# Seven products for eight in a three-stage kernel: blocks 2 and 3 of the second network's first product, and one load queue

## Chip, cores and metric

The kernel runs on one core of a Trainium2 chip. The metric is the device time of one execution in microseconds (us). TensorE (PE) multiplies, VectorE (DVE) and ScalarE (ACT) work on tiles, SyncE (SP) issues transfers (DMAs), GpSimd (POOL) does almost nothing here.

## The reference

Attention with a threshold on 4 x 8 heads of 576 tokens and 64 columns, then two networks on the 2304 tokens of 512 columns. Cut to what is computed:

```python
scores = scale * np.matmul(q, k.transpose(0, 1, 3, 2))
thresh = np.max(scores, axis=-1, keepdims=True) - tau
scores = np.where(scores >= thresh, scores, -1000000000.0)
attn = softmax(scores)
x = (attn @ v)                       # 2304 x 512, float32
h = x @ w_in                         # first network, 512 -> 1024
solu = h * softmax(h)
x = (layernorm(solu) * g_ln) @ w_out # 1024 -> 512
h = x @ w_in2                        # second network, 512 -> 2048
g = np.maximum(h, 0.0) + np.log1p(np.exp(-np.abs(h)))
out = g @ w_out2                     # 2048 -> 512
```

All is float32. The kernel keeps that precision by splitting every operand of the networks into a high and a low part (float32r); a product is three matmuls: high x high, high x low, low x high.

## The kernel before

**Stages.** Attention goes over 32 pairs of heads and tiles of 128 queries: scores (L498), row maximum (L455), exponential (L456), mask with row sum (L458), transposes (L474), product with v (L533). Its result goes into `xr`. The first network goes over nine units of 256 tokens (L668, L726, L727) and stores each unit's result, high and low, to DRAM tensors `x2s` (L733). The weights w_in, w_out of the first network come as 64-bit words and are converted in `convert` by ScalarE (L590) and DVE (L591, L593, L594); for w_in the low half is taken by PE (L614, L615).

**Second network.** The tokens come in five blocks (L737): four of 512 tokens (units 0-1, 2-3, 4-5, 6-7) and one of 256 (unit 8). For each block `m2_load` brings the tokens back from `x2s`; then `m2_chunk` runs over 16 chunks `c` of 128 hidden columns: the first product is 4 parts of the contraction by 3 matmuls into one PSUM bank of tag `h2` (L775), then softplus in four steps on DVE and three on ScalarE (L786 to L792), the high and low half of the result, `gh` and `gl` (L793, L794), and the second product, 3 matmuls for each 128 tokens into the four banks `ys` (L798). With the last chunk `ys` is copied (L815, L817) and stored (L822). `prep_w2` converts the network's weights, one chunk at a time through two buffers `raw2`; `w2t` holds them.

**PSUM.** Eight banks: four of tag `w` and, once attention is over, four of tag `h2`.

**Order of the work.** Every operation is an entry of a plan with what it comes after and the buffers that it takes. For each engine the table `TURNS` lists the entries in the order in which they are issued. A waiting instruction holds up all behind it on its engine, on SP too. `filler` (L396) puts dummy matmuls on PE where a negative number stands in the table.

**Load queues.** `queue` (L410) sends the second half of q and k of pairs 0 and 1 over ScalarE's queue and every other load over SP's; the order on SP is the table's.

Of the kernel before, what the change touches and what calls it, by code (L numbers as in the profile page):

```python
# [957 lines left out]
```

## Time and profile before

| | us |
|---|---|
| median of 3 runs | 914.37 |
| lowest and highest | 912.44, 914.90 |
| the profiled execution | 912.48 |
| its span, first to last instruction | 910.7 |
| PE busy in the span | 894.5 |
| DVE, ACT busy | 689.0, 586.7 |

The span is what the trace covers; 1.8 us of the execution lie outside it. Matmuls are pipelined, so a busy PE is one that has a matmul in it, not one that works at its peak; what a matmul costs in a full stretch is the distance from one start to the next.

### The profile page before, as it was taken

What the parts mean: (1) busy time and instruction counts of PE and PEld (TensorE: products, weight loads), DVE (VectorE), ACT (ScalarE), POOL (GpSimd) and SP (SyncE); (2) the same over time, 40 slices, a digit from 0 to 9 for tenths busy, and PEclk for the clock granted to TensorE, in tenths of its full rate; (3) what the DMA queues carried; (4) which work ended last, traced back from release to release, by engine and by line L of the source; (5) the groups of instructions that cost most, each with busy time, mean ns of one, the idle gap of its engine ahead of it and who ended that gap; (6) DMA issues with size and microseconds to landing.
All of it is one profiled execution on the core that took longest, in us unless ns stands there. A gap on an engine that the chain in (4) does not pass through costs nothing.

```text
span 910.7 us, 14268 instructions
## 1 busy us (share of the span) xinstructions
PE 894.5 (98%) x5388; PEld 703.1 (77%) x5388; DVE 689.0 (76%) x1468; ACT 586.7 (64%) x1153; POOL 0.7 (0%) x6
## 2 busy tenths in 40 slices
PE   5999999999999999999999999999999999999998
PEld 4567776677777777788888888878888888888897
DVE  4899989887877787789879889986465655646566
ACT  4899978887867787757766656654353434444444
POOL 0000000000000000000000000000000000000000
PEclk8999999999999999999999999999999999999999
DMA  8704310131122000164323242431010200200001
GB/s 226 216 3 146 84 30 1 48 101 43 31 73 80 30 24 2 47 208 166 112 83 139 104 153 103 136 104 37 0 46 26 70 0 1 93 1 1 9 27 35
DMA packets 32052, 64.62 MB, mean 71 GB/s; under 512 B 3440, under 2 KB 12912, under 8 KB 31984
## 3 DMA queue, kind: packets, MB, share of 16 engines
q1 hardware_dynamic: 31520, 62.96, 21.5%
q8 instruction: 42, 0.69, 0.3%
q10 hardware_dynamic: 464, 0.75, 0.3%
q14 instruction: 26, 0.21, 0.1%
HBM read 49.55 MB, written 14.16 MB: 70 GB/s over the span
## 4 chain that ended last, share of the span: by engine, by line
PE 86%; DVE 6%; DMA 4%; ACT 3%; issue 1%; SPq 0%; ACTq 0%; DVEq 0%
PE h L775 18%; PE w L798 17%; PE w L668 11%; PE w L474 9%; PE w L533 8%; PE s L498 7%; PE w L726 7%; PE w L727 4%; PE w L709 2%; DMA k<-in_k_dram 1%; PE w L574 1%; DMA raw_out<-in_w_out_dram 1%; DMA raw<-in_w_in_dram 1%; PE w L512 1%; PE s L553 1%; DVE raw_out L593 1%
## 5 line engine op out<-in xcount | busy, mean ns | idle before, releaser
L775 PE MATMUL h<-x2m,w2h 128*128 128x512 f32 (+1 forms) x640 | 181.9, 368 | 0.0
L775 PEld LDWEIGHTS h<-x2m,w2h 128*128 128x128 f32 x640 | 116.8, 188 | 22.1 <-DVE gw L791 0.5
L455 DVE TENSOR_REDUCE nm<-s 128x1 f32<-128x576 f32 x144 | 103.9, 750 | 29.8 <-PE s L498 25.7
L775 PE MATMUL h<-x2m,w2l 128*128 128x512 f32 (+1 forms) x320 | 117.7, 368 | 0.0
L798 PE MATMUL w<-wo2h,gh 128*128 128x512 f32 x288 | 112.4, 390 | 0.5 <-DVE yo L817 0.5
L798 PE MATMUL w<-wo2l,gh 128*128 128x512 f32 x288 | 112.4, 390 | 0.0
L798 PE MATMUL w<-wo2h,gl 128*128 128x512 f32 x288 | 112.1, 389 | 0.0
L458 DVE SCALAR_TENSOR_TENSOR E<-E,etau 128x576 f32<-128x576 f32 x128 | 101.2, 812 | 9.6 <-ACT E L456 8.4
L477 ACT COPY eT<-w 128x512 f32<-128x512 f32 (+1 forms) x186 | 94.0, 544 | 21.9 <-PE w L474 20.8
L456 ACT ACTIVATE E<-s,nm 128x576 f32<-128x576 f32 x128 | 91.6, 747 | 19.7 <-DVE nm L455 19.0
L726 PE MATMUL w<-lhl,wo1h 128*128 128x512 f32 x288 | 103.9, 400 | 0.0
L790 ACT ACTIVATE gw<-gw 128x512 f32<-128x512 f32 (+1 forms) x80 | 47.0, 588 | 63.9 <-DVE t L789 63.5
L794 DVE TENSOR_TENSOR gl<-gw,gh 128x512 fp32r<-128x512 f32 (+1 forms) x80 | 50.8, 635 | 49.0 <-ACT gh L793 48.1
L474 PE MATMUL w<-ident,E 128*128 128x128 f32 x576 | 80.5, 279 | 4.9 <-DVE E L458 2.8
L498 PE MATMUL s<-k,q 64*128 64x288 f32 x512 | 82.5, 438 | 1.2 <-ACT q L424 0.8
L474 PEld LDWEIGHTS w<-ident,E 128*128 128x128 f32 x576 | 62.8, 140 | 26.7 <-issue 7.1
L786 ACT ACTIVATE t<-h 128x512 f32<-128x512 f32 (+1 forms) x80 | 43.9, 552 | 60.1 <-PE h L775 52.6
L793 ACT CAST gh<-gw 128x512 fp32r<-128x512 f32 (+1 forms) x80 | 45.8, 574 | 55.0 <-DVE gw L792 29.2
L727 PE MATMUL w<-lhl,wo1l 128*128 128x256 f32 x288 | 80.8, 280 | 0.0
L533 PE MATMUL w<-eT,v 128*64 128x256 f32 (+1 forms) x680 | 76.3, 371 | 0.0
L791 DVE SCALAR_TENSOR_TENSOR gw<-h,gw 128x512 f32<-128x512 f32 (+1 forms) x80 | 50.8, 636 | 31.0 <-ACT gw L790 30.4
L775 PEld LDWEIGHTS h<-x2m,w2l 128*128 128x128 f32 x320 | 60.2, 188 | 10.1
(107 smaller groups left out, 1544.9 us busy)
## 6 DMA issues: line engine op xcount, KB each, us to landing
x2s<-x SPq DMA_DIRECT2D x36, 256.0 KB, 2.1
x2m<-x2s SPq DMA_DIRECT2D x18, 512.0 KB, 4.9
raw_in<-in_w_in_dram SPq DMA_DIRECT2D x16, 512.0 KB, 3.7
raw_out<-in_w_out_dram SPq DMA_DIRECT2D x16, 512.0 KB, 3.5
v<-in_v_dram SPq DMA_DIRECT2D x16, 320.0 KB, 4.0
q<-in_q_dram SPq DMA_DIRECT2D x30, 144.0 KB, 3.1
raw<-in_w_out_dram SPq DMA_DIRECT2D x4, 1024.0 KB, 6.6
out_dram<-yo SPq DMA_DIRECT2D x15, 256.0 KB, 2.1
```

Of the source, the lines that this page charges most:

```text
L455: mx = op("DVE", 668, 750, lambda: dve.tensor_reduce(out=nm.t, in_=src(), axis=AX.XY, op=ALU.max, negate=True), after=[after], takes=[nm], ...
L456: ex = op("ACT", 638, 741, lambda: act.activation(out=dst().rearrange("p (a b) -> p a b", a=2), in_=src(), func=AF.Exp, bias=nm.t, scale=1.0),
L458: return op("DVE", 739, 900, lambda: dve.scalar_tensor_tensor(out=dst(), in0=dst(), scalar=etau, in1=dst(), op0=ALU.is_ge, op1=ALU.mult, a ...
L474: pe.transpose(bk.t[:, P * i:P * i + P], b_.t[:, c:c + P], ident)
L477: copies.append(op("ACT", occ, occ + 111, lambda: act.copy(out=eT.t[:, 0:width], in_=bk.t[:, 0:width]), after=[g], uses=[bk, eT]))
L498: pe.matmul(s[h].t[:, nh, 0:288], z["q"].t[r, c:c + P], z["k"].t[r, 288 * nh:288 * nh + 288], start=True, stop=True)
L533: pe.matmul(o_.t[64 * h:64 * h + 64, 0:W], z["v"].t[:, vcols(c, h)], e[8 if c == 8 else 4 * h + c](), start=(i == 0), stop=(i == 4))
L668: pe.matmul(ps.t, x__[:, part, :], w_[:, part, 512 * n:512 * n + 512], start=(part == 0 and j_ == 0), stop=(part == 3 and j_ == 2))
L726: pe.matmul(o.t.rearrange("p (a q) -> p a q", a=2), w1t["wo1h"][:, c, P * m:P * m + P], lhl.t[:, :, c, :], start=(c == 0), stop=False)
L727: pe.matmul(o.t[:, 0:256], w1t["wo1l"][:, c, P * m:P * m + P], lhl.t[:, 0, c, :], start=False, stop=(c == 7))
L775: pe.matmul(ps.t[:, 0:n], w2t["in", a, c][:, part, :], x.t[:, b_, part, 0:n], start=(part == 0 and j_ == 0), stop=(part == 3 and j_ == 2))
L798: pe.matmul(ys[j].t, g_.t[:, P * j:P * j + P], w2t["out", a, c], start=(c == 0 and i == 0), stop=(c == NC2 - 1 and i == 2))
```

## The change

**Seven products.** Blocks 2 and 3 (1024 tokens) are no longer taken one after the other. They and the two chunks c and c+8 form a 2 by 2 product in halves of the contraction (256 each). Eight products of such halves become seven, with sums of weights and sums of tokens as operands and five sums of the products behind them. A product is 2 parts by 3 matmuls (`product`). The seven use three `h2` banks, A, B and G: p1 and p2 in A; p6, p7, p4 in B; p5, p3 in G. A copy of p1 (`s1`) is added to B between its products, and results go to SBUF tiles `c22`, `c12` and back into `s1`: p7 comes after the add `u2`, p4 after `u3`, p3 after `c22`. Softplus reads A from PSUM and the other three from SBUF. The second product of block 2 runs beside it; block 3's results are kept in the places of used weights (`keep`) and its second product comes last.

**Sums.** `w2_sums` (DVE, ACT) makes four weight sums for each pair of chunks from the converted weights and stores them, high and low, to DRAM (`wsum`); in the product stage they are loaded again, two loads of 512 KB a pair, into the two `raw2` buffers. `x_sums` makes four token sums from `x2f`, an unsplit copy of the first network's result that units 4 to 7 now store too; one stays in SBUF, three go through `tsum` and come back into the places of weights of chunks 8 to 15 and of block 4's tokens.

**Order.** The blocks come as 0, 1, 4, then 2 and 3 together; block 4 takes its chunks as 8 to 15, then 0 to 7. `queue` sends only q of pair 0 over ScalarE's queue. `TURNS` is new throughout, and so are some constants by which the plan places operations (`LANDS`, `took`, a limit of eight loads under way). Nine tiles of one column (`m_...`) become one tile `few` of nine.

```diff
     def queue(what, i, h=0):
-        return "ACT" if what in "qk" and h and i < 2 else "SP"
+        return "ACT" if what == "q" and i == 0 else "SP"
...
+            if 4 <= u < 8:
+                full.setdefault(u - 4, []).append(load("SP", lambda u=u, m=m: x2f[u - 4][m], lambda xs_=xs_: xs_.t, 128, 1024, after=[s_], uses=[xs_]))
...
+    def four(name, fill, pairs):
+        x = buf("w2b", "sx", f"f_{name}", [P, 4, 256])
...
+        for o_, (i, a, b_, how) in enumerate(pairs):
+            last = [op("DVE", 343, 428, lambda i=i, a=a, b_=b_, how=how: dve.tensor_tensor(out=v(i), in0=v(a), in1=v(b_), op=how), after=last, uses=[x])]
...
+    def halves_of(x, after, into):
...
+            h_ = op("ACT", 110 + 424 * k_, 205 + 425 * k_, lambda src=src, hi=hi: act.copy(out=hi(), in_=src(x.t)), after=after, takes=[own] if new else (), uses=[x] + ([] if new else [own]))
+            got.append(op("DVE", 84 + 518 * k_, 165 + 526 * k_, lambda src=src, hi=hi, lo=lo: dve.tensor_tensor(out=lo(), in0=src(x.t), in1=f(hi()), op=ALU.subtract), after=[h_], uses=[x, own]))
...
+        x, last = four(f"w{c}", fill, [(3, 2, 3, ALU.add), (2, 0, 2, ALU.subtract), (0, 3, 0, ALU.subtract), (1, 1, 0, ALU.subtract)])
...
-    for bi in range(len(blocks)):
-        m2_load(bi, [o_m2] if bi % 2 else [o_w2a])
+    for i in range(2):
+        for j in range(2):
+            x_sums(i, j, [o_w2b])
+    for c in range(8):
+        w2_sums(c, [o_w2b])
+    for bi in (0, 1, 4):
...
+    for c in range(8):
+        sw = [buf("w2a", "raw2", f"sw{c}_{z}", [P, 2, 2, 256], F32R, bufs=2) for z in range(2)]
+        ld = [load("SP", lambda z=z, sw=sw: f(sw[z].t), lambda z=z, c=c: wsum[c][:, 2 * z:2 * z + 2], 128, 4096, after=sw_out[c], takes=[sw[z]]) for z in range(2)]
...
+            for i in range(2):
+                def emit(i=i):
+                    for j_, (a, b_) in enumerate(((0, 0), (0, 1), (1, 0))):
+                        pe.matmul(bk.t, wv(a, i), view(b_, i), start=(first and i == 0 and j_ == 0), stop=(i == 1 and j_ == 2), skip_group_check=not first)
...
+        p1 = product(A_, (0, 0), "b11", [], first=True)
+        o1 = op("ACT", 534, 630, lambda s1=s1, A_=A_: act.copy(out=s1.t, in_=A_.t), after=[p1], takes=[s1], uses=[A_])
+        p6 = product(B_, None, "t2", [], first=True, sum_=0)
+        p2 = product(A_, (0, 2), "b21", [o1])
...
+        u2 = add(hh, B_, s1, [p6, o1, p2] + free_, takes=[hh])
+        p5 = product(G_, None, "t1", [], first=True, sum_=1)
+        p7 = product(B_, None, "t3", [u2], sum_=3)
+        u3 = add(hl, B_, s1, [p7, p2] + free_, takes=[hl])
+        p4 = product(B_, (8, 2), "t4", [u3])
+        c22 = add(hl, G_, hl, [u3, p5])
+        p3 = product(G_, None, "b22", [c22], sum_=2)
+        c21 = add(s1, B_, s1, [p4, u3])
+        c12 = add(hh, G_, hh, [p3, u2])
```

**What the order shows.** First SP's queue at the very start (k0 is k of head pair 0, raw1 a piece of w_in). Before:

```order
L403 DMA q0_105<-in_q_dram 64x576
L403 DMA k0_108<-in_k_dram 64x576
L403 DMA raw1_2_0_121<-in_w_in_dram 128x1024
L403 DMA tau_sb_96<-in_tau_dram 128x1
L403 DMA raw1_0_124<-in_w_in_dram 128x2x1024 x2
L403 DMA k1_127<-in_k_dram 64x576
L403 DMA q1_130<-in_q_dram 64x576
L403 DMA k2_133<-in_k_dram 64x576
```

and in the changed kernel, the loads of pairs 2 and 3 left out after the first of pair 2:

```order
L420 DMA k0_120<-in_k_dram 64x576
L420 DMA k0_120<-in_k_dram 64x640
L420 DMA tau_sb_111<-in_tau_dram 128x1
L420 DMA k1_141<-in_k_dram 64x576
L420 DMA k1_141<-in_k_dram 64x640
L420 DMA q1_144<-in_q_dram 64x576 x2
L420 DMA v0_148<-in_v_dram 128x640
L420 DMA k2_151<-in_k_dram 64x576
```

All of w_in has moved behind the four pairs' q, k and v; q of pair 0 has left SP's queue.

DVE at the same place (nm is a row maximum, E a tile of exponentials that is masked). Before:

```order
L591 TENSOR_SCALAR raw1_2_0_121<-raw1_2_0_121 128x512
L455 TENSOR_REDUCE nm0_0_157<-s0_0_0_136 128x1
L455 TENSOR_REDUCE nm0_1_161<-s0_0_1_137 128x1
L593 SCALAR_TENSOR_TENSOR raw1_2_0_121<-raw1_2_0_121 128x512
L458 SCALAR_TENSOR_TENSOR E0_0_163,sums0_171<-E0_0_163,etau_97 128x576
L591 TENSOR_SCALAR raw1_0_124<-raw1_0_124 128x1024
L458 SCALAR_TENSOR_TENSOR E0_0_163,sums0_171<-E0_0_163,etau_97 128x576
L594 SCALAR_TENSOR_TENSOR raw1_2_0_121<-raw1_2_0_121 128x512
L593 SCALAR_TENSOR_TENSOR raw1_0_124<-raw1_0_124 128x1024
L455 TENSOR_REDUCE nm1_0_208<-s1_0_0_186 128x1
```

and in the changed kernel:

```order
L472 TENSOR_REDUCE nm0_0_170<-s0_0_0_154 128x1
L472 TENSOR_REDUCE nm0_1_175<-s0_0_1_155 128x1
L475 SCALAR_TENSOR_TENSOR E0_0_177,sums0_182<-E0_0_177,etau_112 128x576 x2
L480 TENSOR_SCALAR rinv0_196<-sums0_182 128x2
L472 TENSOR_REDUCE nm1_0_207<-s1_0_0_189 128x1
L472 TENSOR_REDUCE nm1_1_216<-s1_0_1_190 128x1
L475 SCALAR_TENSOR_TENSOR E1_0_218,sums1_227<-E1_0_218,etau_112 128x576 x2
L472 TENSOR_REDUCE nm2_0_249<-s2_0_0_231 128x1
L472 TENSOR_REDUCE nm2_1_259<-s2_0_1_232 128x1
```

Conversions of w_in no longer stand between the softmax steps of the first tiles.

PE in the product stage, from p7 of pair 0 to p4 of it (h2_b0 is pair 0's bank B, sw a loaded weight sum, h2_a1 pair 1's bank A):

```order
L1047 MATMUL h2_b0_8091<-w2l8_4661,sw0_1_8031 128x512
L1047 MATMUL h2_b0_8091<-w2l10_4663,sw0_1_8031 128x512
L1047 MATMUL h2_b0_8091<-w2l14_5712,sw0_1_8031 128x512
L1047 MATMUL h2_b0_8091<-w2l10_4663,sw0_1_8031 128x512
L1047 MATMUL h2_a1_8161<-b11_7445,w2h1_4646 128x512 x2
L1047 MATMUL h2_a1_8161<-b11_7445,w2l1_4647 128x512
L1047 MATMUL h2_b0_8091<-xt4_8118,w2h8_4660 128x512 x2
L1047 MATMUL h2_b0_8091<-xt4_8118,w2l8_4661 128x512
L830 MATMUL w388_7664<-wo2h5_6148,gh4_5_8095 128x512
```

Where one chunk of a block stood at a time, two pairs and the second product of another block now interleave: six matmuls of pair 1 stand between the products p7 and p4 of pair 0.

## Rows read from the trace of the kernel before

**Rows 1.** The page: busy us (share) x instructions, and the main DMA queue.

```profile
PE 894.5 (98%) x5388; PEld 703.1 (77%) x5388; DVE 689.0 (76%) x1468; ACT 586.7 (64%) x1153; POOL 0.7 (0%) x6
...
q1 hardware_dynamic: 31520, 62.96, 21.5%
```

**Rows 2.** The page's chain that ended last: share of the span by engine, by line.

```profile
PE 86%; DVE 6%; DMA 4%; ACT 3%; issue 1%; SPq 0%; ACTq 0%; DVEq 0%
PE h L775 18%; PE w L798 17%; PE w L668 11%; PE w L474 9%; PE w L533 8%; PE s L498 7%; PE w L726 7%; PE w L727 4%; PE w L709 2%; DMA k<-in_k_dram 1%; PE w L574 1%; DMA raw_out<-in_w_out_dram 1%; DMA raw<-in_w_in_dram 1%; PE w L512 1%; PE s L553 1%; DVE raw_out L593 1%
```

**Rows 3.** A piece of that chain in order of time: start, us, what.

```profile
680.93 4.08 PE h L775 x18
```

**Rows 4.** Groups by line and shape, PE: count, busy us, mean ns, idle before.

```profile
L775 PE MATMUL h<-x2m,w2h 128*128 128x512 f32 x512 | 158.0, 390 | 0.0
```

**Rows 5.** Stretches: length, busy us of PE, PEld, DVE, ACT, POOL, clock, DMA.

```profile
0.00:42.08 42.08, 31.59 (x138) 19.65 (x139) 26.70 (x49) 26.26 (x43) 0.70 (x6) 0.88 0.86 239
500.00:560.00 60.00, 60.00 (x295) 50.51 (x294) 52.53 (x105) 38.54 (x75) 0.00 (x0) 1.00 0.37 128
560.00:720.00 160.00, 159.48 (x703) 131.13 (x702) 110.99 (x187) 78.88 (x138) 0.00 (x0) 1.00 0.19 63
720.00:850.00 130.00, 130.00 (x576) 107.71 (x575) 74.18 (x121) 56.96 (x98) 0.00 (x0) 1.00 0.05 17
```

**Rows 6.** The same view, two short stretches of the start.

```profile
16.00:18.00 2.00, 1.05 (x2) 0.17 (x2) 2.00 (x3) 0.00 (x0) 0.00 (x0) 0.73 1.05 179
18.00:20.00 2.00, 0.00 (x0) 0.00 (x0) 1.21 (x3) 0.92 (x1) 0.00 (x0) 0.50 1.08 192
```

**Rows 7.** Timeline of the start, ACT, SP, PE: start, us, what [idle before].

```profile
0.73 0.57 ACTq L403 DMA_DIRECT2D q<-in_q_dram  x1
4.31 1.28 ACT L424 ACT_TABLE_LOAD   x1 [4.31 <-DMA q<-in_q_dram]
6.72 0.31 ACT L407 ACTIVATE minus<-ident 128x128 fp32r<-128x128 f32 x1 [0.44 <-issue]
9.74 0.74 ACT L456 ACTIVATE E<-s,nm 128x576 f32<-128x576 f32 x1 [0.43 <-DVE nm L455]
...
2.25 0.60 SPq L403 DMA_DIRECT2D raw<-in_w_in_dram  x1
...
12.35 1.24 PE L498 MATMUL s<-k,q 64*128 64x288 f32 x8
20.90 0.80 PE L615 MATMUL w<-w1h,minus 128*128 128x512 f32 x1 [3.85 <-ACT w1h L605]
22.11 1.47 PE L498 MATMUL s<-k,q 64*128 64x288 f32 x3 [0.41 <-DMA v<-in_v_dram]
```

**Rows 8.** Timeline of DVE, 31 to 44 us.

```profile
33.55 1.29 DVE L594 SCALAR_TENSOR_TENSOR raw<-raw 128x512 uint32<-128x512 uint32 x2
38.85 0.69 DVE L591 TENSOR_SCALAR raw<-raw 128x1024 uint32<-128x1024 uint32 x1
42.08 1.42 DVE L455 TENSOR_REDUCE nm<-s 128x1 f32<-128x576 f32 x2 [0.25 <-PE s L498]
```

**Rows 9.** Groups by line and shape, DVE.

```profile
L794 DVE TENSOR_TENSOR gl<-gw,gh 128x512 fp32r<-128x512 f32 x64 | 44.1, 688 | 44.5 <-ACT gh L793 44.0
L788 DVE TENSOR_SCALAR gw<-t 128x512 f32<-128x512 f32 x64 | 27.1, 423 | 29.2 <-ACT t L787 28.1
L730 DVE TENSOR_TENSOR x2s<-w,x2s 128x256 f32<-128x256 f32 x36 | 15.1, 421 | 11.0 <-ACT x2s L729 10.5
```

**Rows 10.** Line L403 from 540 to 600 us, 16 loads.

```profile
DMA to landing us min/median/max: 3.4/3.6/7.4
```

**Rows 11.** Timeline of the end, the last two stores.

```profile
907.39 0.35 ACTq L811 DMA_DIRECT2D out_dram<-yo  x1
907.84 0.34 SPq L811 DMA_DIRECT2D out_dram<-yo  x1
```

More of the change, by code (lines that the diff above doesn't have):

```diff
@@ L24 @@
 NET = 8
+LAST = 3
 NE = 4
@@ L269, in ready @@
                     k = need[b.tag] = need.get(b.tag, 0) + 1
-                    if len(slots[b.tag]) < k or b.tag != "w" and b.turn != taken[b.tag] + k:
+                    if len(slots[b.tag]) < k or b.tag not in ANY and b.turn != taken[b.tag] + k:
                         return None
@@ L341, in tile_attention_solu_softplus @@
     x2s = [dram.tile([4, P, 2, 256], F32, tag=f"x2s{u}", name=f"x2s{u}") for u in range(len(UNITS))]
+    x2f = [dram.tile([4, P, 256], F32, tag=f"x2f{u}", name=f"x2f{u}") for u in range(4)]
+    tsum = [dram.tile([P, 2, 2, 512], F32, tag=f"tsum{i}", name=f"tsum{i}") for i in range(3)]
+    wsum = [dram.tile([P, 4, 2, 256], F32, tag=f"wsum{c}", name=f"wsum{c}") for c in range(8)]
     pools = dict(psW=psW, m1=m1, xs=xs, w1=w1, psS=psS, at=at)
     stacks = dict(m1=ph1, xs=xs_stack, w1=w1_stack, at=att_stack)
-    done = plan_of(nc, ctx, sb, const, ident, minus, pools, stacks, w1t, x2s, q, k, v, tau, w_in, w_out, g_ln, w2_in, w2_out, out).order()
+    done = plan_of(nc, ctx, sb, const, ident, minus, pools, stacks, w1t, x2s, (x2f, tsum, wsum), q, k, v, tau, w_in, w_out, g_ln, w2_in, w2_out, out).order()
     with tc.manual_schedule():
@@ L369, in items_of, with plan_of @@
     return items
-def plan_of(nc, ctx, sb, const, ident, minus, pools, stacks, w1t, x2s, q, k, v, tau, w_in, w_out, g_ln, w2_in, w2_out, out):
+def plan_of(nc, ctx, sb, const, ident, minus, pools, stacks, w1t, x2s, sums2, q, k, v, tau, w_in, w_out, g_ln, w2_in, w2_out, out):
     PSUM = bass.MemoryType.PSUM
@@ L797, in emit @@
                 for i, (g_, a) in enumerate(((gh, "h"), (gh, "l"), (gl, "h"))):
-                    pe.matmul(ys[j].t, g_.t[:, P * j:P * j + P], w2t["out", a, c], start=(c == 0 and i == 0), stop=(c == NC2 - 1 and i == 2))
-            y = last_y[bi, j] = op("PE", 681, 850, emit, after=[a8, a9, last_y.get((bi, j))] + wready["2out", c] + behind, takes=[ys[j]] if c == 0 else (), uses=[gh, gl] + ([] if c == 0 else [ys[j]]), mode="G")
-            if c == NC2 - 1:
+                    pe.matmul(ys[j].t, g_.t[:, P * j:P * j + P], w2t["out", a, c], start=(first and i == 0), stop=(last and i == 2))
+            y = last_y[bi, j] = op("PE", 681, 850, emit, after=[a8, a9, last_y.get((bi, j))] + wready["2out", c] + behind, takes=[ys[j]] if first else (), uses=[gh, gl] + ([] if first else [ys[j]]), mode="G")
+            if last:
                 yo = buf("m2", "yo", f"yo{bi}_{j}", [P, DM], bufs=2)
-                if bi == len(blocks) - 1 and j == n // P - 1:
+                if bi == LAST and j == n // P - 1:
                     for e, lo_, c_ in (("ACT", 0, 256), ("DVE", 256, 512)):
@@ new lines, in plan_of, with w2_sums, fill @@
+    readers = {}
+    def w2_sums(c, behind):
+        def fill(x):
+            got = []
+            for i in range(2):
+                got.append(op("DVE", 602, 691, lambda i=i: dve.tensor_tensor(out=x.t[:, 2 * i:2 * i + 2, :], in0=f(w2t["in", "h", c + 8 * i]).rearrange("p (a b) q -> p a (b q)", a=2), in1=f(w2t["in", "l", c + 8 * i]).rearrange("p (a b) q -> p a (b q)", a=2), op=ALU.add),
+                              after=wready["2in", c + 8 * i] + behind, takes=[x] if i == 0 else (), uses=[x] if i else ()))
+            readers["s", c] = got
+            return got
+        x, last = four(f"w{c}", fill, [(3, 2, 3, ALU.add), (2, 0, 2, ALU.subtract), (0, 3, 0, ALU.subtract), (1, 1, 0, ALU.subtract)])
+        sw_out[c] = []
+        for i in range(2):
+            g = buf("w2a", "raw2", f"g_w{c}_{i}", [P, 2, 2, 256], F32R, bufs=2)
+            low = halves_of(x, last, [(lambda t, i=i: t[:, 1:3, :] if i else t[:, 0::3, :], lambda g=g: g.t[:, :, 0, :], lambda g=g: g.t[:, :, 1, :], 512, g, True)])
+            sw_out[c].append(load("SP", lambda i=i: wsum[c][:, 2 * i:2 * i + 2], lambda g=g: f(g.t), 128, 4096, after=low, uses=[g]))
@@ new lines, in x_sums, with fill @@
+    def x_sums(i, j, behind):
+        def fill(x):
+            return [load("SP", lambda z=z: x.t[:, z:4:2, :], lambda z=z: x2f[2 * z + j][i:4:2].rearrange("c p q -> p c q"), 256, 1024, after=full[2 * z + j] + behind, takes=[x] if z == 0 else (), uses=[x] if z else ()) for z in range(2)]
+        x, last = four(f"x{i}{j}", fill, [(0, 1, 0, ALU.subtract), (1, 3, 1, ALU.subtract), (3, 3, 0, ALU.subtract), (2, 2, 3, ALU.subtract)])
+        q_ = slice(256 * j, 256 * j + 256)
+        new = "t1" not in xt_
+        if new:
+            xt_["t1"] = buf("w2b", "xd", "xt1", [P, 2, 2, 512], F32R)
+        t1 = xt_["t1"]
+        t1_ready.extend(halves_of(x, last, [(lambda t: t[:, 0], lambda: t1.t[:, 0, i, q_], lambda: t1.t[:, 1, i, q_], 256, t1, new)]))
+        g = buf("w2a", "raw2", f"g_x{i}{j}", [P, 2, 2, 256], F32R, bufs=2)
+        low = halves_of(x, last, [(lambda t: t[:, 1::2, :], lambda: g.t[:, :, 0, :], lambda: g.t[:, :, 1, :], 512, g, True)])
+        for z in range(2):
+            ts_out.append(load("SP", lambda z=z: tsum[z][:, :, i, q_], lambda z=z: f(g.t[:, z]), 256, 1024, after=low, uses=[g]))
+        g4 = buf("w2a", "raw2", f"g4_x{i}{j}", [P, 2, 2, 256], F32R, bufs=2)
+        low = halves_of(x, last, [(lambda t: t[:, 2], lambda: g4.t[:, 0, 0, :], lambda: g4.t[:, 0, 1, :], 256, g4, True)])
+        ts_out.append(load("SP", lambda: tsum[2][:, :, i, q_], lambda: f(g4.t[:, 0]), 256, 1024, after=low, uses=[g4]))
@@ L864, in plan_of, with two_chunks @@
             o.behind.append(scores[max(0, round(REL[i]))])
-    last_h, stored = [], {}
+    last_h, stored, full = [], {}, {}
     for u, un in enumerate(units):
         m1_unit(u)
+    def two_chunks(pool_, a, c):
+        t = w2t["two", a, c // 2 - 4] = pool_.tile([P, 2, 4, P], F32R, tag=f"w2{a}{c}", name=f"w2{a}{c}")
+        for i in range(2):
+            w2t["in", a, c + i] = t[:, i]
     def close_at():
@@ new lines, in plan_of @@
+    pair = {}
+    for name, pool_, tag, u0, m in (("b11", "m2x", "xbh", 4, 0), ("b21", "m2x", "xbl", 4, 2), ("b22", "w2a", "xal", 6, 2)):
+        x = buf(pool_, tag, name, [P, 2, 2, 512], F32R)
+        got = []
+        for j in range(2):
+            for a in range(2):
+                got.append(load("SP", lambda a=a, j=j, x=x: f(x.t[:, a, :, 256 * j:256 * j + 256]), lambda a=a, j=j, u0=u0, m=m: x2s[u0 + j][m:m + 2, :, a, :].rearrange("c p q -> p c q"), 256, 1024,
+                                after=stored[u0 + j] + [o_w2b], takes=() if got else [x], uses=[x] if got else ()))
+        pair[name] = [x], got, lambda a, i, x=x: x.t[:, a, i, :]
@@ new lines, in plan_of @@
+    t1 = xt_["t1"]
+    pair["t1"] = [t1], t1_ready, lambda a, i: t1.t[:, a, i, :]
+    for name, z, al in (("t2", 1, "h"), ("t3", 0, "l")):
+        got = []
+        for a in range(2):
+            for i in range(2):
+                k_ = 2 * a + i
+                got.append(load("SP", lambda al=al, k_=k_: f(w2t["two", al, k_][:, :, 0:2, :]).rearrange("p c a b -> p c (a b)"), lambda z=z, a=a, i=i: tsum[z][:, a, i, :].rearrange("p (c q) -> p c q", c=2), 256, 1024,
+                                after=ts_out + [readers["in", 8 + 2 * k_], readers["in", 9 + 2 * k_]] + readers["s", 2 * k_] + readers["s", 2 * k_ + 1]))
+        pair[name] = [], got, lambda a, i, al=al: w2t["two", al, 2 * a + i][:, :, 0:2, :].rearrange("p c a b -> p c (a b)")
@@ L906, in plan_of @@
+    ys = [bank() for _ in range(4)]
+    for n, (c, g, done_) in enumerate(kept):
+        m2_out(3, c, n == 0, n == 15, g, done_, ys, [o_w2b])
     return plan
```

125 lines of the change are left out of this document (90 added, 35 removed), and 252 rows, old and new, of the table TURNS.

## The prediction

> **What bounds the kernel now.** I read the page first: PE is busy 98% of the span, VectorE (DVE) 76% [rows 1]. A busy PE is modelled, so I went on to the chain that ended last: 86% of it is PE, and the second network's two products, L775 and L798, are its largest lines with 18% and 17% [rows 2]. In the chain's pieces, 18 matmuls of L775 follow each other in 4.08 us, 226.7 ns each, with no gap [rows 3]; the 390 ns that a group shows as one matmul's mean [rows 4] overlaps the next ones, so only the spacing is a price. The stage table then says where PE is full: 60.00 of 60, 159.48 of 160 and 130.00 of 130 us in the three stretches from 500 to 850, while DVE falls from 88% busy to 57% [rows 5]. So from 500 us on a matmul taken away is time taken away, as long as nothing else becomes late. Only the start is different: in the first 42.08 us PE is busy 31.59 (filler matmuls included) and DVE 26.70 [rows 5], PE sits idle 3.85 us before L615 [rows 7], and the granted clock is 0.50, the lower level of 1.2 GHz, at 18 to 20 us, where PE did nothing after 1.05 busy us in the two before [rows 6].
>
> **The products.** Before, blocks 2 and 3 take for each pair of chunks (c, c+8) four products of 4 parts by 3 matmuls, 48; after, seven products of 2 parts by 3, 42. Eight pairs: 48 matmuls of 128x512 fewer. The order of the two kernels says the same: L775 stands 960 times before, and after it 576 on the old line and 336 on the new one, 912. No other matmul goes; 864 second products stay. 48 x 226.7 ns = **-10.9 us**, all of it on the path, since the rows are from a stretch without gaps [rows 3]. The Trainium skill's page "TensorE: Matmul & The Clock Gate", section "Back-to-back issue gap", gives about 131 ns for an N=512 matmul in a real stream of weight loads and matmuls; by that price the removal is worth 6.3 us and the time would be 4.6 us later than the sum below. The rows here show 226.7, so the page's price isn't used and gets no chance.
>
> **What is added beside it.** Weight sums: for a pair two adds of 512 columns, four of 256, two low halves of 512 on DVE. Back to back, two 512-column operations of 0.69 take 1.29 us, so one occupies 0.60 [rows 8]; by the same overlap of 0.09 a 256-column one (0.42) occupies 0.33, and so does L788 (0.42) [rows 9]. That is 3.7 us a pair, 30 us for eight; the four token sums add 6 x 0.33 + 0.60 = 2.6 us each, 10 us. They stand between the middle of block 0 and block 4, where DVE has 49 us idle in 560 to 720 alone [rows 5]: 40 us cost nothing if they are spread, and the order does interleave them with the softplus steps. ScalarE has more room there (78.88 of 160 busy [rows 5]). The sums go through DRAM: 16 stores of x, 12 and 16 stores of sums, 16 loads of weight sums and some 20 of token sums, about 27 MB on 63 MB that take 21.5% of the DMA engines [rows 1]; bandwidth hides them, and SP, which issues each in about 0.35 us [rows 11], has some 80 more to issue in 910 us. What the SP queue can cost is a late landing, which is a rival below.
>
> **The stage of the seven products.** Of a pair PE has 42 + 24 matmuls (the second product of block 2), 66 x 226.7 = 15.0 us. DVE has 5 adds, 4 softplus of one short and three long operations, and two low halves: 19 x 0.60 + 4 x 0.33 = 12.7 us, 85%. Before, the same engine was 88% busy in 500 to 560 while PE showed 60.00 of 60 [rows 5], so this load alone doesn't stall PE. New is that the adds stand inside a product's bank: p7 waits for u2, p4 for u3, p3 for c22. Between p7 and p4 the order leaves 6 to 15 other matmuls, 1.4 to 3.4 us, for the end of a matmul (0.39 less 0.23, 0.16 us), an add (0.69) and what DVE has in front of it (one operation, 0.60): 1.45 in all. The cover just does. If it fails by one operation at each of the 24 adds that a product waits for, that is 24 x 0.25 to 0.3 = 6 us; if it holds, 0; a gain is excluded, since the matmuls are counted already. I take **+2**, nearer to the stretch where PE had no gap at a like DVE load.
>
> **The start.** Before, ScalarE's and SP's queues each issue half of pair 0 at 0.73, then w_in goes in at 2.25; the exponentials of tile 0 begin at 9.74, scores of tile 1 start at 12.35 and those of tile 2 at 22.11 [rows 7]. After, SP issues k0, then tau, then pairs 1 to 3 with v, and w_in last; q0 stands on ScalarE's queue behind a table load (1.28 us) and the minus copy (0.31) [rows 7]. q0 is so issued about 1.6 us later, and before the first exponentials ScalarE now also scales q1, queued behind it: the first exponentials can't be earlier than before. But tiles 1 and 2 no longer wait behind 2.6 MB of weights. The two DVE orders reach the same point, the row maxima of the sixth tile (42.08 before [rows 8]), with the same weights converted and one mask of 0.74 us less. Up to there DVE was idle 42.08 - 26.70 = 15.4 us, 8.6 of it before its first instruction. The first wait stays; of the other 6.8 perhaps half goes. Best: the point is bounded by w_out's first part (its first DVE step at 38.85 before [rows 8]), whose buffer is w_in's, and by 26 us of work after 8.6 to 9.5: **-5.5**. Worst: w_in lands later than the work for it is due, +1. I take **-3**, nearer to the best, because less work is listed before the same point. What follows is as before: PE and DVE both nearly full.
>
> **The end.** Before, the last block's last tile is one store on each queue, 907.39 and 907.84 [rows 11]; after, it is the tile of tails, two stores of 64 rows each: one more issue of 0.35 us. **+0.35**. The matmuls that end the kernel are the 192 of block 3's second product, 43.5 us with DVE at 16 x 0.60 us only.
>
> **Sum.** The profiled execution took 912.48 us, 1.8 more than its span. 912.48 - 10.9 + 2 - 3 + 0.35 = 900.9. It lies 1.9 under the median of 914.37 and among the lowest of the runs shown, so I add half of that: **902**. The forecast's own ends: 912.48 - 10.9 - 5.5 + 0.35 = 896.4, and 912.48 - 10.9 + 6 + 1 + 0.35 = 908.9 without, 910.8 with, the whole offset.
>
> **Rivals.** (1) *The start brings nothing*: the clock falls to 0.50 as before, or the maxima of the sixth tile stay at 42. For it: ScalarE's new order. Against: tiles 1 and 2 have their data some 5 to 10 us earlier. 902 + 3 = **905**.
> (2) *DVE becomes the bound of the product stage.* If each operation held the engine for its full duration, a pair would be 19 x 0.69 + 4 x 0.42 = 14.8 us against PE's 15.0; at the 88% that DVE reached in its fullest stretch [rows 5] a pair takes 16.8, 1.85 more, 14.8 us for eight in place of my +2: 902 + 12.8 = **914.8**, no difference. Against it: two operations in 1.29, not 1.38 [rows 8]. The Trainium skill's page "VectorE: DVE Perf Modes", section "The DRAIN you can't avoid", says that the next operation can't issue until the pipe has emptied, which is this rival's premise; the trace's pair in 1.29 us disagrees with it for these rows.
> (3) *The loads of the weight sums come late, and the kernel gets slower.* Only two buffers hold them, four products a pair read them, and p6 and p7 of the next pair wait for the next load. From the last matmul that reads a buffer to the first that needs the load after it the order leaves, at 14 places, 18 matmuls three times, 21 twice, then 24, 27, 30, 33 twice and more: 4.1, 4.8, 5.4, 6.1, 6.8 us. Loads of 512 KB on L403 landed after 3.4 to 7.4 us, median 3.6 [rows 10]. At 3.6 nothing waits; at 7.4 each time the places lose 3 x 3.3 + 2 x 2.6 + 2.0 + 1.3 + 0.6 = 19 us, and 902 - 2 + 19 = **919**. It decides the sign from about 6.7 us. Against it: half of the rows lie at 3.4 to 3.6, and SP's queue holds little in this stage but these loads and four stores.
> (4) *The start at its best*: 902 - 2.5 = **899.5**. That the products aren't fewer is no rival, as the order shows.
>
> **How the numbers follow.** Forecast (898 to 908) 0.70, rival 1 0.13, rival 2 0.07, rival 3 0.06, rival 4 0.04. Predicted is 902. The range leaves out rivals 2 and 3: 897 to 909.5. A difference under 0.3%, 2.7 us, can't be told from none here. Faster: the forecast, 1, 4 and a small part of 2, 0.89; same: 2, 0.05; slower: 0.06.
>
> **What would show it.** The new product line 336 times at 226 to 228 ns of spacing in the chain. PE's idle time and waits in the product stage under 4 us, DVE there about 85% busy: step and cover right; long waits of the new line for the adds: rival 2; for the sums' loads, with landings over 6 us: rival 3. Maxima of the sixth tile at about 39 instead of 42.08, and the first exponentials still at 9.5 to 10.5: the start right. If that point is at 42 or later, the start's term is wrong; if PE stays without gaps and the time is still over 909, a stage that I hold unchanged (first network, block 0) has lost what the products gained.

## The result and the profile after

The changed kernel takes 902.32 us (median of 4 runs, 901.8 to 903.12) against 913.68 for the kernel before (912.44 to 914.9): a ratio of 0.9876, with a 95% interval from 0.9859 to 0.9894. The profiled execution took 901.94 us with a span of 900.1. The prediction was 902.0. The total is right; the terms under it are not all right, and the experiments below are mostly about those. Of all executions below one, of the kernel whose loads come late, took 2237.79 us, with matmuls at about twice their length, and is left out of its median.

The page of the kernel after: busy time by engine, the main DMA queue, and the chain that ended last by engine and line, to be held against [rows 1, 2].

```profile
PE 885.9 (98%) x5356; PEld 696.6 (77%) x5356; DVE 749.9 (83%) x1600; ACT 606.8 (67%) x1189; POOL 0.7 (0%) x6
...
q1 hardware_dynamic: 45536, 89.51, 29.9%
...
PE 89%; DVE 4%; DMA 3%; ACT 2%; issue 1%; SPq 0%; DVEq 0%; ACTq 0%
PE w L830 20%; PE h L797 12%; PE w L685 10%; PE w L491 8%; PE s L515 8%; PE w L550 7%; PE w L739 7%; PE w L740 4%; PE h_b L1047 4%; PE h_a L1047 2%; PE h_g L1047 2%; PE w L722 2%; PE w L591 1%; DMA raw<-in_w_in_dram 1%; PE w L529 1%; DVE nm L472 1%
```

PE is still what the chain consists of. 32 matmuls fewer in all: 48 of the products went, 16 dummy ones of 128x128 came. DVE has 61 us more, and its share of the chain falls, from 6% to 4%; L1047 has taken the place of a third of L775. Two pieces of that chain in order of time, in the stage of the seven products (start, us, what):

```profile
736.49 1.36 PE h_b L1047 x6
737.85 1.36 PE w L830 x6
```

1.36 us for six is 226.7 ns, the spacing of [rows 3]. The stretches (length, busy us of PE, PEld, DVE, ACT, POOL, clock, DMA), which answer [rows 5]:

```profile
0.00:37.45 37.45, 31.68 (x177) 21.88 (x178) 26.58 (x50) 27.28 (x45) 0.70 (x6) 0.95 0.81 259
500.00:560.00 60.00, 59.44 (x291) 49.69 (x290) 53.35 (x109) 36.61 (x73) 0.00 (x0) 1.00 0.42 144
560.00:718.00 158.00, 158.00 (x768) 133.18 (x768) 149.93 (x303) 95.21 (x187) 0.00 (x0) 1.00 0.46 157
742.00:842.00 100.00, 100.00 (x442) 82.61 (x441) 92.68 (x158) 58.54 (x100) 0.00 (x0) 1.00 0.22 74
```

In the stage of the sums (560 to 718) DVE is 95% busy and PE has no gap; in the stage of the products (742 to 842) DVE is 93% busy, not the 85% of the prediction, and PE has no gap there either. The start, in the timeline, for [rows 7, 8], and the clock in three stretches, for [rows 6]:

```profile
0.73 1.28 ACT L424 ACT_TABLE_LOAD   x1 [0.73 <-PEq L1121]
1.34 1.22 ACTq L420 DMA_DIRECT2D q<-in_q_dram  x2
9.27 1.35 ACT L473 ACTIVATE E<-s,nm 128x576 f32<-128x576 f32 x2
13.55 1.88 PE L515 MATMUL s<-k,q 64*128 64x288 f32 x8 [0.51 <-ACT E L473]
...
37.45 1.41 DVE L472 TENSOR_REDUCE nm<-s 128x1 f32<-128x576 f32 x2
```

```profile
18.00:20.00 2.00, 1.17 (x8) 0.61 (x8) 1.43 (x4) 1.94 (x4) 0.00 (x0) 0.94 1.02 408
20.00:22.00 2.00, 2.00 (x20) 1.78 (x18) 1.31 (x3) 1.83 (x3) 0.00 (x0) 0.50 1.05 414
22.00:24.00 2.00, 1.64 (x22) 1.35 (x20) 1.97 (x3) 1.34 (x4) 0.00 (x0) 0.71 1.01 399
```

The scores of tile 2 start at 13.55 instead of 22.11, the sixth tile's maxima at 37.45 instead of 42.08, and in these two executions the clock is at its lower level for 3.4 us instead of 10.2. The loads of the weight sums (issue to landing: lowest, median, highest of 16) and the end, for [rows 10, 11]:

```profile
DMA to landing us min/median/max: 3.5/3.7/5.7
```

```profile
895.35 0.39 PE L830 MATMUL w<-wo2h,gl 128*128 128x512 f32 x1
...
896.18 1.16 ACTq L844 DMA_DIRECT2D out_dram<-yo  x2
896.18 0.42 DVE L839 COPY yo<-w 128x256 f32<-128x256 f32 x1 [1.70 <-ACT yo L837]
896.63 1.11 SPq L844 DMA_DIRECT2D out_dram<-yo  x2
```

**A measure for what follows.** "Lead" is PE's progress beside that of the kernel before: all matmuls started up to a time, dummies left out, each counted at the usual spacing of its shape, in one kernel less the other. Worked out so from the two traces, the changed kernel is 3.2 us ahead at 60 us, 1.9 at 80, 1.6 at 160, 1.9 at 400, 0.7 at 525, and 0.3 at its last matmul: 906.56 - 895.35 = 11.21, of which the missing products are 48 x 0.2267 = 10.88. From the last matmul to the end it takes 4.80 us, 0.67 more than before. 10.88 + 0.33 - 0.67 = 10.54 is the difference of the two profiled times. So the start did gain what was predicted, and nearly all of it was gone at the end; the product stage cost nothing.

### The profile page after: what moved, and what is told of

Same layout as the page of the kernel before. It is cut to its first block, busy times and chain, and to the rows that moved or that the text cites. A ratio compares the mean times of both kernels' runs of the same rounds, so it can differ in the third digit from the quotient of the medians.

```text
span 900.1 us, 14551 instructions
## 1 busy us (share of the span) xinstructions
PE 885.9 (98%) x5356; PEld 696.6 (77%) x5356; DVE 749.9 (83%) x1600; ACT 606.8 (67%) x1189; POOL 0.7 (0%) x6
## 4 chain that ended last, share of the span: by engine, by line
PE 89%; DVE 4%; DMA 3%; ACT 2%; issue 1%; SPq 0%; DVEq 0%; ACTq 0%
PE w L830 20%; PE h L797 12%; PE w L685 10%; PE w L491 8%; PE s L515 8%; PE w L550 7%; PE w L739 7%; PE w L740 4%; PE h_b L1047 4%; PE h_a L1047 2%; PE h_g L1047 2%; PE w L722 2%; PE w L591 1%; DMA raw<-in_w_in_dram 1%; PE w L529 1%; DVE nm L472 1%
## 5 line engine op out<-in xcount | busy, mean ns | idle before, releaser
L494 ACT COPY eT<-w 128x512 f32<-128x512 f32 (+2 forms) x186 | 94.4, 544 | 19.6 <-PE w L491 18.5
L550 PEld LDWEIGHTS w<-eT,v 128*64 128x64 f32 x680 | 45.9, 140 | 28.3 <-ACT eT L494 7.1
L515 PEld LDWEIGHTS s<-k,q 64*128 64x128 f32 x512 | 46.7, 186 | 23.7 <-ACT E L473 7.7
L739 PEld LDWEIGHTS w<-lhl,wo1h 128*128 128x128 f32 x288 | 54.1, 188 | 13.0 <-issue 0.8
L830 PEld LDWEIGHTS w<-wo2h,gl 128*128 128x128 f32 x288 | 54.1, 188 | 11.5
L830 PEld LDWEIGHTS w<-wo2h,gh 128*128 128x128 f32 x288 | 54.2, 188 | 10.1
L830 PEld LDWEIGHTS w<-wo2l,gh 128*128 128x128 f32 x288 | 54.2, 188 | 10.1
L685 PE MATMUL w<-w1h,xh 128*128 128x512 f32 x144 | 60.1, 417 | 0.0
L685 PE MATMUL w<-w1h,xl 128*128 128x512 f32 x144 | 56.6, 393 | 0.0
L685 PE MATMUL w<-w1l,xh 128*128 128x512 f32 x144 | 56.3, 391 | 0.0
```

The lines of the kernel that those rows point to most:

```text
L494: copies.append(op("ACT", occ, occ + 111, lambda: act.copy(out=eT.t[:, 0:width], in_=bk.t[:, 0:width]), after=[g], uses=[bk, eT]))
L515: pe.matmul(s[h].t[:, nh, 0:288], z["q"].t[r, c:c + P], z["k"].t[r, 288 * nh:288 * nh + 288], start=True, stop=True)
L550: pe.matmul(o_.t[64 * h:64 * h + 64, 0:W], z["v"].t[:, vcols(c, h)], e[8 if c == 8 else 4 * h + c](), start=(i == 0), stop=(i == 4))
L685: pe.matmul(ps.t, x__[:, part, :], w_[:, part, 512 * n:512 * n + 512], start=(part == 0 and j_ == 0), stop=(part == 3 and j_ == 2))
L739: pe.matmul(o.t.rearrange("p (a q) -> p a q", a=2), w1t["wo1h"][:, c, P * m:P * m + P], lhl.t[:, :, c, :], start=(c == 0), stop=False)
L830: pe.matmul(ys[j].t, g_.t[:, P * j:P * j + P], w2t["out", a, c], start=(first and i == 0), stop=(last and i == 2))
```

## Experiments

Each ratio is to the kernel before as it ran beside the run in question (medians 912.66 to 913.31). Where a run is set against the changed kernel, its median is compared with the 902.32 above, which comes from another session, so a difference of 1 us or less says nothing.

### What is the start worth, and where does its gain go?

The orders of both kernels pass points at which every engine has the same set of steps behind it, so that the first part of one order can be put before the rest of the other. Two points are used: DVE's 88th step (70.1 us before, 66.3 after) and its 181st (124.9 and 123.3). What changes is the numbers in `TURNS`, up to the point or between the points, dummies included (22 calls in the new start, 14 in the old), and with the start one line, here from the new start to the old; for the kernel before with the new start it is the other way round:

```diff
-        return "ACT" if what == "q" and i == 0 else "SP"
+        return "ACT" if what in "qk" and h and i < 2 else "SP"
```

**The changed kernel with the old start.**

> The changed kernel with the start of the kernel before: the load queues of before, and on each engine before's order up to a point that both orders reach with the same set of steps done (its 88th step on VectorE, at 70.1 us before, 66.3 after); from there on the changed order. Theory A (what the start gains reaches the end unless a later order gives it back): the 3.8 us of lead at that point are lost, 902.3 + 3.8 = 906.1. Theory B (a later bound takes the gain away whatever the order): 902.3 within 1. The product stage is untouched under both.

Measured: 910.26 us (12 runs, 907.37 to 916.3), ratio 0.9971 to the kernel before (0.9952 to 0.9991); 8 us later than the changed kernel, more than either theory said. Part of it is not the start but the seam: DVE, which has little idle time between 40 and 100 us in either kernel, waits at the join for a part of w_out (DVE's waits from 64 to 74 us: total, times, longest), and PE has its gap right after, from 72 to 76:

```profile
DVE raw L608 <- DMA raw<-in_w_out_dram: 1.7, 1, 1.7
```

```profile
72.00:76.00 4.00, 3.23 (x22) 1.38 (x20) 4.00 (x6) 3.32 (x5) 0.00 (x0) 1.00 0.28 113
```

The lead falls from 0.7 at 66 us to -2.5 at 100. That the join causes this is an argument from these rows. The run says that the old start costs something, not how much.

**The kernel before with the new start.**

> The other way round: the kernel before with the changed kernel's load queues and order up to the same point, eight products as before. Theory A: 913.7 - 3.8 = 909.9. Theory B: 913.7 within 1.

Measured: 910.34 us against 912.94, ratio 0.9965 (0.9951 to 0.9978): 2.6 us faster by the medians. The product stage is the old one, so this is the start by itself: queues, order and dummies together, which no run takes apart. First and last start of the first network's second product (line, operation, duration, first to last start) in the kernel before and in this one:

```profile
L726 PE MATMUL w<-lhl,wo1h x288: 387/395/501, 187.2 to 526.2; 128*128 128x512 f32 x144
```

```profile
L726 PE MATMUL w<-lhl,wo1h x288: 387/395/497, 184.5 to 523.5; 128*128 128x512 f32 x144
```

2.7 us ahead at both ends, and the last matmul of the kernel is at 903.2 instead of 906.6. With the old order behind it, the gain stays. Theory A holds.

**The new order up to the second point.**

> The kernel before with the changed order and queues up to the 181st step of VectorE (124.9 us before, 123.3 after; a lead of 1.6). Theory A, that the changed order itself gives 2.2 us of the start's gain back between the 88th and the 181st step: 913.7 - 1.6 = 912.1, later than the run with the new start alone by 2.2. Theory B: 913.7, and the same as the run with the new start alone.

Measured: 910.97 us, ratio 0.9970 (0.9957 to 0.9983), 0.6 later than the run before this one where theory A said 2.2. The same rows give 185.3 and 524.2, 0.8 and 0.7 later. The sign is A's, the size a third of it; the two times cannot be told apart.

**The changed kernel with the old order between the points.**

> The changed kernel with before's order only between the two points (88th to 181st step of VectorE): new start, old order to 120 us, new order after it. Theory A: the lead of 3.8 is kept where it fell to 1.6, 902.3 - 2.2 = 900.1, faster than both kernels. Theory B: 902.3 within 0.6.

Measured: 902.24 us (901.13 to 904.1), ratio 0.9875 (0.9857 to 0.9893), the same as the changed kernel: theory B, as far as times go. The same line in the changed kernel and in this one:

```profile
L739 PE MATMUL w<-lhl,wo1h x288: 387/395/500, 185.5 to 526.9; 128*128 128x512 f32 x144
```

```profile
L739 PE MATMUL w<-lhl,wo1h x288: 387/395/500, 184.4 to 525.8; 128*128 128x512 f32 x144
```

In these two traces the middle is 1.1 us better, to the end of this stretch; the medians don't show it. But in both the advance on the kernel before shrinks between the first and the last of these matmuls, from 1.7 to -0.7 and from 2.8 to 0.4, where the old order (the run with the new start alone) kept 2.7. Part of that is only a shift, since the new order has begun block 0's products earlier; in lead, which counts those, it falls from 1.9 to 0.7 and from 2.9 to 1.7 between 400 and 525 us, against 2.5 and 2.5 with the old order. So the new order of that stretch gives back some 1.2 us. The run without sums on DVE, below, loses the same 1.2 there (0.7 to -0.5), so it isn't the sums' load on DVE. Which of the moved steps does it, or whether the added stores and loads do, wasn't tried.

**Dummies in the start's gaps.**

> The changed kernel with before's order in the middle of attention, as in the earlier run (902.2), and 9 more dummy matmuls of 128x128 in the two gaps of PE at 19 and 22.2 us. If PE's gaps there are what lets the granted clock fall to 0.50 at 20 to 30 us in some executions: no fall, the executions closer together, 902.2 - 1 = 901.2. If not: 902.2 to 902.6 and the same spread of 3 us.

Measured: 901.96 us (6 runs, 900.52 to 902.67), ratio 0.9871 (0.9844 to 0.9898). The granted clock was 1.00 in every stretch from 14 to 34 us. It proves nothing, though: it was 1.00 in that stretch in the run before this one, which differs by these dummies alone, and in four of the runs below as well. The time is not to be told from the changed kernel's.

### What is a product worth, and what is next behind PE?

**Eight products again.**

```diff
+                    if x == "b11" and i == 0:
+                        for ii in range(2):
+                            for j_, (a, b_) in enumerate(((0, 0), (0, 1), (1, 0))):
+                                pe.matmul(bk.t, wv(a, ii), view(b_, ii), start=(ii == 0 and j_ == 0), stop=(ii == 1 and j_ == 2))
```

> The changed kernel with the product p1 computed twice for each pair, so that a pair has eight products again: 48 matmuls of 128x512 more, everything else as it was. Prediction's theory (a product is worth its matmuls, no cover is lacking): 902.3 + 48 x 0.2267 = 913.2. Rival (VectorE or the loads bound the product stage, PE has room): less than 902.3 + 6 = 908.

Measured: 913.83 us (10 runs), ratio 1.0013 (1.0000 to 1.0026) to the kernel before. That is 11.5 above the changed kernel, where the matmuls alone make 10.9. With as many matmuls as before, the whole of the rest of the change, sums, loads, adds and the new order, is worth nothing or up to 2.4 us of loss. The product is all that the change gains.

**Six products.**

```diff
+                    if x == "b22":
+                        return
```

> The changed kernel without the matmuls of p3, six products a pair; that part of the result is left out. 48 matmuls less: 60 x 0.2267 = 13.6 us of PE for a pair beside 12.7 us of VectorE. Prediction's theory (cover of 1.45 us does, VectorE at 93% still hides): 902.3 - 10.9 = 891.4, at most 2 above it. Rival (VectorE is next and near): a pair takes 12.7 / 0.88 = 14.4 us, 0.8 more than 13.6, 8 x 0.8 = 6.6 us of the 10.9 lost: 898.

Measured: 900.78 us, ratio 0.9869 (0.9853 to 0.9885): 1.5 us of the 10.9. Neither figure held, and the prediction's was far off. The stretch of the stage, and PE's waits in it (us in total, times, longest; the lines of this kernel stand two further down, L1049 for L1047):

```profile
742.00:842.00 100.00, 95.96 (x412) 76.17 (x411) 94.13 (x161) 59.76 (x103) 0.00 (x0) 1.00 0.21 69
```

```profile
PE h_b L1049 <- DVE c L1062: 2.2, 3, 1.1
PE h_a L1049 <- ACT s L1057: 1.6, 2, 1.2
```

PE now waits for the adds (c) and for ScalarE's copy of p1 (s). In the changed kernel PE waits for neither a single time. The chain that ended last says the same: between 742 and 842 us it is PE to 100% in the changed kernel, and DVE to 72%, ScalarE to 16%, PE to 6% here, most of it softplus steps in which DVE and ScalarE wait for each other. How near that was can be worked out from the starts: a product begins 0.74 us after the start of the add it waits for when it really waits. At the 16 places (p7 behind u2, p4 behind u3) the smallest distance is 0.98 in the changed kernel, a margin of 0.24 us; with six products it is 0.74 at four places.

**Two operations more on DVE.**

```diff
-            return op("DVE", 640, 720, lambda: dve.tensor_tensor(out=out_.t, in0=ps.t, in1=in_.t, op=ALU.add), ...)
+            return op("DVE", 640, 720, lambda: [dve.tensor_tensor(out=out_.t, in0=ps.t, in1=in_.t, op=ALU.add) for _ in range(2 if takes else 1)], ...)
```

> The changed kernel with the two adds u2 and u3 of each pair done twice (same inputs, same result): 16 VectorE operations of 0.69 more, 0.60 each where they follow another, 1.2 us a pair, and each of p7 and p4 has one more operation ahead of it. Theory C (VectorE with its chains to ScalarE needs nearly as long for a pair as PE's 15.0, as the run with six products showed): a pair becomes 15.0 + 1.0, 902.3 + 8 = 910. Theory D (VectorE has the 15% of room that the sum 19 x 0.60 + 4 x 0.33 = 12.7 says, the six products were bound by something else): 902.3, at most 1.5 more.

Measured: 910.64 us, ratio 0.9978 (0.9960 to 0.9996): 8.3 above the changed kernel, as theory C said. The stage, and PE's waits from 700 us to the end:

```profile
742.00:852.00 110.00, 106.16 (x450) 84.33 (x449) 102.98 (x173) 59.36 (x101) 0.00 (x0) 0.98 0.20 67
```

```profile
PE h_b L1047 <- DVE c L1060: 3.2, 5, 1.8
```

DVE is 94% busy, and the distance from add to product is at its least, 0.74 to 0.75, at six of the 16 places. The chain in this stretch is DVE to 69%, ScalarE to 12%, PE to 14%. The edit does two things at once: it loads DVE, and it puts an operation into the chain from p6 to p4. Their shares of the 8.3 us can't be told apart by it, and about 1.5 us in this trace are matmuls at the lower clock, which stood at 0.50 for 3.4 us after a wait of PE.

**Six products with less on DVE.**

```diff
-        a9 = op("DVE", ..., lambda: dve.tensor_tensor(out=v(gl), in0=v(g), in1=f(v(gh)), op=ALU.subtract), ...)
+        a9 = op("DVE", ..., lambda: act.copy(out=v(gl), in_=v(g)) if bi == 2 else dve.tensor_tensor(out=v(gl), in0=v(g), in1=f(v(gh)), op=ALU.subtract), ...)
```

> Six products as in the earlier run, and the low halves of block 2's results written by ScalarE as a plain copy (that part of the result is left out): 2 x 0.60 = 1.2 us a pair less on VectorE, no matmul more or less. Theory C (VectorE bounds six products): 900.8 - 8 x 1.1 = 892, near the 891.4 that the matmuls alone would give. Theory D (a latency between PE and the banks, or ScalarE, bounds it): 900.8 within 1.5.

Measured: 898.36 us, ratio 0.9834 (0.9804 to 0.9864). 2.4 us came, where C asked for 9 and D for none. The stage, and PE's waits from 700 us to the end (the two shortest left out):

```profile
742.00:842.00 100.00, 96.70 (x420) 77.80 (x419) 87.45 (x148) 67.09 (x118) 0.00 (x0) 1.00 0.21 69
```

```profile
PE h_b L1049 <- DVE c L1062: 1.6, 2, 0.9
PE h_a L1049 <- ACT s L1057: 1.6, 2, 1.2
PE h_b L1049 <- DMA xt<-tsum: 1.1, 1, 1.1
```

DVE is down to 87% and PE still waits at the same places. The edit isn't clean: the copies go to ScalarE (59.76 to 67.09 busy), for which PE waits too. The chain of the stage goes from 72% DVE and 6% PE to 32% DVE, 16% ScalarE and 50% PE. So six products are held up by DVE together with its exchanges with ScalarE; how much of that is load and how much the length of the chain, these runs don't separate. It is an argument only that the left-out matmuls of p3 are also missing as cover between the other products.

### Do the sums cost anything?

**The sums off DVE.**

```diff
-            last = [op("DVE", 343, 428, lambda ...: dve.tensor_tensor(out=v(i), in0=v(a), in1=v(b_), op=how), ...)]
+            last = [op("DVE", 343, 428, lambda: None, ...)]
...
-            got.append(op("DVE", ..., lambda ...: dve.tensor_tensor(out=lo(), in0=src(x.t), in1=f(hi()), op=ALU.subtract), ...))
+            got.append(op("DVE", ..., lambda ...: act.copy(out=lo(), in_=src(x.t)), ...))
```

(and the two additions of the weights' halves in `w2_sums` likewise become one copy each on ScalarE).

> The changed kernel with the weight and token sums taken off VectorE: the additions and subtractions are left out, and ScalarE writes a copy of an operand in their place, so the stores and loads stay. VectorE has some 40 us less in the stretch of 550 to 720 us. Prediction's theory (the sums cost nothing beside the matmuls): 902.3 within 0.7. Rival (VectorE's 95% in that stretch causes PE's waits there, 0.9 us at 550 to 560): 901.3 or less.

Measured: 903.15 us, ratio 0.9892 (0.9873 to 0.9911): no gain. The stage of the sums:

```profile
560.00:718.00 158.00, 157.99 (x765) 132.97 (x764) 113.32 (x215) 115.16 (x232) 0.00 (x0) 1.00 0.47 157
```

DVE falls from 149.93 busy to 113.32, and PE is as full as it was. 37 us of DVE were free. The stores and loads of the sums are still there and the copies load ScalarE (95.21 to 115.16), so the run speaks of DVE's part.

**The loads of the weight sums late.**

```diff
-        ld = [load("SP", lambda z=z, sw=sw: f(sw[z].t), lambda z=z, c=c: wsum[c][:, 2 * z:2 * z + 2], 128, 4096, ...) for z in range(2)]
+        ld = [op("SP", 620, None, lambda z=z, sw=sw, c=c: [sp.dma_start(out=f(sw[z].t), in_=wsum[c][:, 2 * z:2 * z + 2]) for _ in range(2)], ...) for z in range(2)]
```

> The changed kernel with each load of weight sums in the product stage issued twice in a row into the same buffer, its reader waiting for both. If the two go one after the other they land after about 7.4 us instead of 3.7, by the prediction's formula for the 14 places with 18 matmuls and more between (4.1, 4.8, 5.4, ... us): 902.3 + 19 = 921. If they overlap, about 5.0 us: 3 x 0.9 + 2 x 0.2 = 3 us, 905. If the loads have slack that the formula doesn't see: 902.3.

Measured: 948.36 us (3 runs, 943.79 to 949.18), ratio 1.0377 (1.0343 to 1.0412). The kernel was run again for its rows.

> The kernel with each load of weight sums issued twice once more, for its rows: 944 to 949 again. If the second load of a pair is issued only when the first has landed, each load stays 3.7 us and SP's queue is held meanwhile, so that the loads behind it go out late too, which the prediction's formula left out; if both go out at once, the landing of the second is what is late.

Measured: 946.83 us, 44.5 above the changed kernel. SP's queue (start, us, what), PE's waits, and two stretches:

```profile
719.61 5.24 SPq L1038 DMA_DIRECT2D sw<-wsum  x2
724.90 0.43 SPq L420 DMA_DIRECT2D w2l<-tsum  x1
725.42 5.49 SPq L1038 DMA_DIRECT2D sw<-wsum  x2
730.96 0.43 SPq L420 DMA_DIRECT2D w2h<-tsum  x1
```

```profile
PE h_b L1047 <- DMA sw<-wsum: 19.4, 7, 4.1
PE h_b L1047 <- DMA w2h<-tsum: 6.3, 1, 6.3
PE h_b L1047 <- DVE tp L812: 1.8, 1, 1.8
```

```profile
760.00:800.00 40.00, 32.64 (x120) 25.96 (x120) 24.50 (x42) 15.94 (x28) 0.00 (x0) 0.83 0.36 121
800.00:840.00 40.00, 32.37 (x122) 25.80 (x123) 27.04 (x46) 17.95 (x31) 0.00 (x0) 0.87 0.35 114
```

SP waits between the two loads of a pair, the second goes out 4.9 us after the first, and the load of the token sum behind it (`w2h`) goes out late too. The Trainium skill's page "DMA: Bandwidth & Descriptors", section "Two DMAs through the same engine are not ordered", says to make the issuing engine wait for the first transfer's semaphore before it issues one that depends on it; SP does so here, with two issues in 5.24 us. The prediction's 19 us is near what PE waits for these loads themselves, 19.4, but the loads also queue behind each other here, which its formula doesn't have, so the agreement may be chance. It left out two things: what is queued behind on SP, 6.3 us, and the clock, which PE's gaps bring down to a mean of 0.83 to 0.91 over 160 us. By the starts of the matmuls from 718 to 895 us, nine gaps at full clock, in which those waits lie, cost 29 us, and the wider spacing of the matmuls at the lower level costs 14: together 43 of the 44.5.

## The prediction, step by step

- **Products, -10.9.** Right: the spacing is the same on the new line (1.36 us for six), and putting 48 matmuls back costs 11.5 us, which agrees with 10.9 within the scatter of the two medians. The estimate of 6.3 us from the 131 ns that the Trainium skill's page "TensorE: Matmul & The Clock Gate", section "Back-to-back issue gap", gives is refuted by the same run.
- **Sums cost nothing.** Right for DVE: 37 us taken off it in their stage moved the time by nothing, and PE shows 158.00 of 158 there.
- **Product stage, +2.** Mis-sized: 0. PE shows 100.00 of 100. The rule set 1.45 us against a cover of 1.4 to 3.4; its smallest, six matmuls, is 1.36 and should have failed by a little, but the tightest place measured has 0.24 us to spare. DVE's share was underrated, 93% for 85%: the sum gave each long operation 0.60, as if the next always began before it ended, but 63 of the 157 operations from 742 to 842 us aren't overlapped by the next one and take their whole 0.69 or 0.42. 34 of the 63 are followed by one that waits for DVE itself (below).
- **Start, -3.** The size is right, a little low where it was worked out: the maxima of the sixth tile come 4.6 us earlier (37.45, not about 39), PE's lead is 3.2 us at 60 us, and the start alone, in the kernel before, is worth 2.6. The step that failed is the sentence after it, "What follows is as before": it isn't. The changed kernel loses 1.2 between 60 and 80 us (the run with the old order there 0.7) and as much again between 400 and 525, and 0.3 is left at the end. Six executions with the new order lose 2.5 to 3.3 us of lead between 60 and 525 us, the one with the old order behind the new start 0.5; which of the moved steps costs it stays open. Of details: the first exponentials came at 9.27, 0.47 earlier, where I had said that they could not. The premise was wrong that q0's issue would stand behind the table load: it went out at 1.34, while the table load ran to 2.01.
- **End, +0.35.** 0.67 in the trace: each queue issues two stores, and the last issue ends 0.77 us later behind the last matmul than before, where I had counted 0.35.
- **Offset, +1.** The median lies 0.4 above the profiled execution.
- **Sum.** -10.9 + 2 - 3 + 0.35 was -11.55; the trace has -10.88 - 0.33 + 0.67 = -10.54. The forecast was met to 0.3 us by luck: two errors of 2.0 and 2.7 us had opposite signs.
- **Rivals.** The first (the start brings nothing, 905) is nearly what was left at the end, but not for its reason: the maxima of the sixth tile came 4.6 us earlier; its time misses by the +2 as well. The second (DVE bounds the stage) didn't come, but was nearer than 0.07 says: two operations more on DVE a pair cost 8.3, one product fewer a pair brings only 1.5, and in both runs the chain goes through DVE. The third had the right mechanism and half the price: 946.8 and not 919, with the loads that late; as they are, landing after 3.7 us, PE waits for none.

## What to carry to other kernels

A product taken from a PE that is full is worth its spacing, once; count what the next product would be worth before going on, since here taking out the eighth was worth 11 us and taking out one more, with the order left as it was, 1.5. A gain at the start is only a gain at the end if the order behind it is left alone: put the new start before the old rest to see what it is worth by itself. Price a late load with what is queued behind it and with the clock that the gaps cost, not with its own wait alone.
